# A spectral block with a gated feed-forward layer on one core: filter copies shared out anew, shift columns on ScalarE, special unit and inverse tables moved

## The chip, the core and the metric

One core of a Trainium2 chip. The metric is device time in microseconds (us) of one execution; the median of several runs stands for a kernel. A profile is of one execution, and its span runs from its first to its last instruction. Engines are named as the profile does: PE (TensorE matmul), PEld (its weight loads), DVE (VectorE), ACT (ScalarE), POOL (GpSimd), SP (SyncE, which here only issues DMAs).

## What is computed

With x of 2048 rows and 640 columns, a row c and its modulation vectors sa, ca, ga, sb, cb, gb:

```
sa, ca, ga, sb, cb, gb = split(silu(c) @ w_mod, 6)
h = layernorm(x) * (1 + ca) + sa
x = x + ga * irfft2(rfft2(h) * (w_r + 1j * w_i))
h = layernorm(x) * (1 + cb) + sb
x = x + gb * ((silu(h @ w_gate) * (h @ w_up)) @ w_down)
```

The spectral filter has 2048 x 321 complex values; w_gate and w_up are 640 x 1728, w_down is 1728 x 640. Everything comes and goes as bfloat16.

## The kernel before

The order of the work is written out by hand: each engine runs its instructions in the order in which the Python code issues them, and waits are put in where tiles depend on each other. So moving a line of Python moves an instruction on its own engine's queue.

**Front** (lines 253 to 483). x, the tables and the filters are loaded. The rows are normalized in eight steps t of two tiles (`bn`, `rstd_of`, `normed` on DVE; `normed_pool`, L374, on POOL for the steps and halves that `NP` lists, after `shift` has made a bias). `tok(t)` (L383) transforms along the rows on PE, ACT copies the result out (L386), `ddft(t)` (L324, L327) transforms along the columns, and ACT copies that (L400) into A. One reciprocal square root per step (L359) runs on POOL. `pool_w` issues the eight big filter loads (L276) on POOL's DMA queue: real and imaginary, two column halves, and two directions, `dm` 0 and 1. DMAs of the tables K and the modulation weights are issued by ACT at the end of steps 6 and 7 (L478).

**The filter tile** Wt holds, in each half of 64 partitions (`dm`), 32 partitions that were loaded and 32 partitions that `w_rev` (L319) fills with the same rows, columns reversed. A call takes an engine, `dm` and a range lo to hi of the 82 columns, over all 128 rows k. The calls before: POOL, `dm` 1, 24 to 48; DVE, both, 48 to 64; DVE, both, 64 to 82; DVE, `dm` 0, 0 to 24; ACT, `dm` 0, 24 to 48; DVE, `dm` 1, 0 to 24.

**Groups** (lines 489 to 712). A is turned around in groups of four columns l: groups 0 to 3 are columns 48 to 63, group 4 is column 80 alone (`iE`), then columns 4 to 47 four at a time with the special group 12 (`iS`, "S") among them, group 17 is columns 0 to 3, and groups 18 to 21 are columns 64 to 79; NG is 22. Groups 0 to 4 come through PE transposes (`t2_pe`, copies L530), the others through five DMA transposes on SP (`t2_dma`, L511). `stage_a(g)` makes two matmuls (L542) into one of three pairs of PSUM banks and multiplies both halves by the filter: groups in `MIX` have ACT copy the second half out (L549), DVE multiply the first (L550) and POOL the second (L551); the others are one DVE instruction of twice the size (L553). `stage_c(g)` makes the inverse matmuls (L632, eight for a group of four, in bank g % 2), which ACT copies to E (L633; DVE for groups in `DEV`). The loop at line 688 runs, for round g, `stage_a(g + 2)` and then `stage_c(g - 2)`.

**The special unit** handles row 0 and the Nyquist row. `col0` (L506) has POOL gather one column of each turned group into `Bc`, by the schedule `CZ`; `sa_cols` and `sa_rows` make the shift's own transform; `special_a` (L560, L561) needs all of `Bc`, and the filter's last row k = 127; `special_c` (L570, ACT copy L572) issues four POOL DMAs (L575, L576) into E. `ga_mod` (L638, L643) makes the broadcast ga; `mods` (L580) makes three vectors of modulation columns. After the loop, `s1em` (L653) and `s1er` (L663) transform back along the rows, with the table H, and L1160 and L1163 along the columns with the table RI, which DVE multiplies by ga first (L709, L712). The feed-forward layer follows (lines 715 to 1248).

`idle_pe` (L302) issues matmuls whose result nobody reads.

Of the kernel before, what the change touches and what calls it, by code (L numbers as in the profile page):

```python
# [21 lines left out]
RW = 164  # L22
# [145 lines left out]
def adaln_block_kernel(ctx, tc, A_x, A_w_r, A_w_i, B_x, B_w_gate, B_w_up, B_w_down, c, w_mod, out):  # L168
# [110 lines left out]
    def pool_w(i, n):  # L279
        for ci, mm, dm in wsets[i:i + n]:  # L280
            load_w(nc.gpsimd, ci, mm, dm, *((P - 1, 128, P, -1) if dm else (0, 1, P - 1)))
# [32 lines left out]
                nc.tensor.matmul(ps_ap[:, w * c5:w * c5 + w], lhsT=lhsT, rhs=sc_col[:, k:k + 1].to_broadcast([P, w]),  # L314
                                 start=(k == 0 and c5 == 0), stop=(k == NC5 - 1 and c5 == NC5 - 1))

    def w_rev(eng, dm, lo, hi):
        src = Wt[64 * dm:64 * dm + 32]
        (eng.copy if eng is nc.scalar else eng.tensor_copy)(Wt[64 * dm + 32:64 * dm + 64, :, lo:hi],  # L319
                                                            bass.AP(tensor=src.tensor, offset=src.offset + 160 - lo, ap=[list(src.ap[0]), [RW, P], [-1, hi - lo]]))  # L320

    def dft_d(zps, lhs):
        for h in range(2):
# [6 lines left out]
    if True:  # L330
        CS = (4, 0, 1, 2, 3)
        BA = (1, 3, 5, 7, 11)
        NP = {4: (0,), 5: (0,), 6: (0, 1), 7: (0,)}

        def bn(T, stats=True, aggr=True):
            for k in range(2 * stats):
# [118 lines left out]
        for t in range(2, NS):  # L455
            tok(t)
            if t == 2:
                ddft(0)
            for T in (2 * t + 4, 2 * t + 5):
                if T < NT and T not in BA:  # L460
                    bn(T)
                if T == 2 * t + 4 and t < 7:
                    if t + 1 in NP:
                        shift(t + 1)
                    normed(t + 1, [h for h in range(2) if h not in NP.get(t + 1, ())])
            if t < 7:
                normed_pool(t + 1, NP.get(t + 1, ()))
            if t == 2:
                bn_act(11)
            if t < 5:  # L470
                pool_w(*((4, 2), (6, 1), (7, 1))[t - 2])
            if t < 6:
                rstd_of(t + 2)
            if t == NS - 1:
                idle_pe(3, 4, 3)
            ddft(t - 1)
            for o, i in late.get(t, ()):
                nc.scalar.dma_start(o, i)  # L478
        ddft(7)
        idle_pe(3, 4, 7)  # L480
        w_rev(nc.gpsimd, 1, 24, 48)
        for dm in range(2):
            w_rev(nc.vector, dm, 48, 64)


    Em = rE.cut(0, [64, 128])
# [15 lines left out]
    if True:  # L502
# [11 lines left out]

        for i in range(5):
            t2_dma(i)
        for i in range(1, 4):
            nc.sync.dma_start(wm_r[:, :, i, :], wm_m[:, :, i, :])
        nc.sync.dma_start(Htab[:], H_dram)
        nc.sync.dma_start(RI[:], RI_dram)  # L520
        Wd_sb = rA.cut(0, [NFC, D])

        def t2_pe(slot):
# [68 lines left out]
        def sa_cols(bank):  # L592
            mps = psum[:, bank, 330:330 + NC5]
            mod_cols(mps, wm_sa)
            nc.vector.tensor_copy(sa_col[:], mps)  # L595
            nc.gpsimd.tensor_scalar_mul(sa4[:], mask4[:], sa_col[:, 4:5])
            nc.gpsimd.tensor_copy(_rev(SL, 0, [[257, 4], [132, 2], [16, NS]]),
                                  sa_col[:, 0:4].unsqueeze(2).unsqueeze(3).to_broadcast([P, 4, 2, NS]))
            nc.gpsimd.tensor_copy(_rev(SL, 1024, [[1, 4], [132, 2], [16, NS]]),
                                  sa4[:].unsqueeze(2).unsqueeze(3).to_broadcast([P, 4, 2, NS]))  # L600
# [43 lines left out]


        def s1b(t):
            return 6 if t == 1 else 2 if t == 0 or t % 2 else 4

        def s1em(t, rs=range(4)):
            vps = banks(s1b(t), 2, [8, 128])  # L650
# [13 lines left out]
                                 rhs=Htab[:, t, v, :], start=(v == 0), stop=(v == 1))  # L664
            return vt_copy(t, lo, 5)

        MIX = {g: True for g in range(1, NG - 2) if g % 5 in (1, 2, 4) and g not in (iE, iS)}
        DEV = {NG - 2}
        CZ = {4: (0, 8), 6: (8, 16), 8: (24, 16), 9: (40, 8), 10: (64, 16)}
        PPs = {}  # L670
        t2_pe(0)
        t2_pe(1)
# [1 line left out]
        t2_pe(2)  # L674
        t2_pe(3)
        PPs[1] = stage_a(1)
        w_rev(nc.vector, 0, 64, 82)
        w_rev(nc.vector, 1, 64, 82)
        PPs[2] = stage_a(2)
        sa_cols(0)  # L680
        for s in range(4):
            col0(B2of[groups[s][0]][0], slice(groups[s][0], groups[s][0] + 4)) if s < 3 else None
        B2 = B2of[60][0]
        col0(B2[:, 0:4], slice(60, 64))
        col0(B2[:, 4:5], slice(80, 81))
        w_rev(nc.vector, 0, 0, 24)
        w_rev(nc.scalar, 0, 24, 48)
        for g in range(1, NG + 2):
            if g in CZ:
                l0, n = CZ[g]  # L690
                col0(B2of[l0][0], slice(l0, l0 + n))
            if g + 2 < NG:
                PPs[g + 2] = stage_a(g + 2)
            if g == 1:
                w_rev(nc.vector, 1, 0, 24)
            if g in (3, 4):
                ga_mod(320 * (g - 3), 0)
            if g == 8:
                load_wd()
            if g > 1:  # L700
                stage_c(g - 2)
            if g - 2 == iE:
                sa_rows(iE % 2)
            if g - 2 == iS:
                mods(1, iS % 2)
            if g in (NG - 2, NG - 1):
                mods(g - NG + 4, 2 + 2 * ((g + 2) % 3))
        s1em(0)
        nc.vector.tensor_tensor(RI[:, 1], RI[:, 1], ga_bc[:], ALU.mult)  # L709
        vt_copy(0, 0, 4)  # L710
        s1em(1)
        nc.vector.tensor_tensor(RI[:, 0], RI[:, 0], ga_bc[:], ALU.mult)  # L712
        gdiag = rL.cut(10496, [NC5, 128])

    Wgu = rW.cut(0, [2, NC5, 13 * 128])
# [582 lines left out]
```

## Time and profile before

| | us |
|---|---|
| median of 3 runs | 257.44 (256.94 to 257.88) |
| the profiled execution's own time | 257.12 |
| its span | 255.3 |
| PE busy in the span | 237.0 (93%) |
| DVE busy | 206.8 (81%) |
| ACT busy | 170.2 (67%) |
| POOL busy | 76.0 (30%) |
| mean granted clock of PE | 0.986 |
| front, to the first `t2_pe` matmul (L528) | 0 to 35.73 |
| groups, to the first `s1er` matmul (L663) | 35.73 to 72.11 |
| the rest | 72.11 to 255.3 |

The busy times of engines lie beside each other and do not add up to the span. In the page's second part the span is cut into 40 slices of 6.4 us; a digit is the busy share in tenths, and PEclk is the clock that PE was granted, in tenths. A row of the timeline is start, length, engine, line, operation, output and inputs, how many were merged, and in brackets the time for which the engine stood idle before it and what ended that. A row of stretches gives a window, its length, then busy time and number of instructions of PE, PEld, DVE, ACT and POOL, the granted clock, the DMA engines' busy share and GB/s.

### The profile page before, as it was taken

The page shows a single profiled execution, that of the slowest core. Times are in us where ns is not written, and L with a number is a line of the kernel's source. Part 1 is how long each engine was busy: PE and PEld are TensorE (multiplying, and loading weights), DVE is VectorE, ACT ScalarE, POOL GpSimd, SP SyncE. Part 2 cuts the span into 40 slices and gives each one's busy share as a digit, 9 for nine tenths or more (in the row PEclk, how much of TensorE's full clock was granted, in tenths as well). Part 3 has the DMA queues.
Part 4 walks back from the last instruction along what each step waited for, and adds up shares of the span by engine and source line. Part 5 has one row for each costly group of instructions (what it writes and reads, how often), then busy time and mean ns, then how long its engine had stood idle before and what let it go on. Part 6 is the DMA issues. An engine that isn't in the chain of part 4 may idle for free.

```text
span 255.3 us, 5627 instructions
## 1 busy us (share of the span) xinstructions
PE 237.0 (93%) x2100; PEld 179.4 (70%) x2100; DVE 206.8 (81%) x469; ACT 170.2 (67%) x329; POOL 76.0 (30%) x98
## 2 busy tenths in 40 slices
PE   8678784978999999999999999999999999999994
PEld 2467652556899888778888768888775665656773
DVE  3997379866768999698998996778998788879874
ACT  5988756365789879939876287876336777775220
POOL 4598544464633533200200440000442000003410
PEclk9999999599999999999999999999999999999999
DMA  6999969999998999920000511310511000000111
GB/s 186 347 302 168 161 206 281 168 377 383 209 303 158 282 272 284 181 67 3 0 4 0 103 54 53 25 30 0 105 53 51 3 0 0 4 0 0 55 51 51
DMA packets 40445, 31.78 MB, mean 124 GB/s; under 512 B 22401, under 2 KB 37218, under 8 KB 40290
## 3 DMA queue, kind: packets, MB, share of 16 engines
q1 hardware_dynamic: 35760, 22.35, 32.4%
q0 software_dynamic: 2912, 6.94, 13.3%
q10 hardware_dynamic: 1746, 2.14, 2.8%
q8 instruction: 16, 0.26, 0.4%
q14 instruction: 11, 0.09, 0.1%
HBM read 24.03 MB, written 2.62 MB: 104 GB/s over the span
## 4 chain that ended last, share of the span: by engine, by line
PE 81%; DVE 3%; POOL 2%; ACT 2%; issue 2%; DVEq 0%; POOLq 0%; ACTq 0%
PE psum L1019 35%; PE psum L890 18%; PE psum L989 6%; PE psum L632 3%; PE psum L867 3%; PE psum L653 3%; PE psum L542 3%; PE psum L1160 2%; PE psum L1163 2%; PE psum L977 2%; DVE rW L319 1%; PE psum L638 1%; PE psum L383 1%; POOL rE L551 1%; PE psum L580 1%
## 5 line engine op out<-in xcount | busy, mean ns | idle before, releaser
L1019 PEld LDWEIGHTS <-rW 128*128 128x128 bf16 (+1 forms) x429 | 42.0, 98 | 12.6
L1019 PE MATMUL psum<-rW 128*128 128x256 bf16 (+1 forms) x247 | 42.2, 287 | 0.0
L916 POOL TENSOR_TENSOR rM<-rM,rL 128x320 f32<-128x320 f32 x6 | 5.4, 906 | 96.6 <-ACT rL L915 96.6
L890 PEld LDWEIGHTS <-rE 128*128 128x128 f16 (+1 forms) x196 | 19.0, 97 | 7.8
L890 PE MATMUL psum<-rE 128*128 128x320 f16 (+1 forms) x147 | 22.9, 299 | 0.0
L1057 ACT COPY rX<-psum 128x384 f32<-128x384 f32 (+2 forms) x27 | 14.0, 519 | 7.5 <-PE psum L1019 7.4
L1050 ACT COPY rH<-psum 128x384 f32<-128x384 f32 (+2 forms) x27 | 13.9, 516 | 7.0 <-PE psum L1019 6.3
L1019 PEld LDWEIGHTS <-rE 128*128 128x128 f16 x156 | 15.2, 98 | 4.7
L1054 DVE TENSOR_TENSOR rH<-psum,rM 128x512 bf16<-128x512 f32 (+1 forms) x24 | 15.0, 624 | 4.1 <-PE psum L1019 2.2
L1073 ACT ACTIVATE rL<-psum 128x384 bf16<-128x384 f32 (+2 forms) x27 | 14.4, 532 | 5.5 <-PE psum L1019 3.4
L1058 DVE TENSOR_TENSOR rX<-psum,rX 128x384 f32<-128x384 f32 (+2 forms) x27 | 16.3, 604 | 1.6 <-ACT rX L1057 1.4
L1044 ACT COPY rM<-psum 128x384 f32<-128x384 f32 (+2 forms) x27 | 13.9, 514 | 4.0 <-PE psum L1019 3.9
L633 ACT CAST rE<-psum 127x512 bf16<-127x512 f32 x19 | 11.1, 591 | 7.2 <-PE psum L632 5.7
L632 PEld LDWEIGHTS <-rE 128*128 128x128 bf16 x160 | 11.5, 116 | 6.2 <-issue 3.2
L551 POOL TENSOR_TENSOR rE<-rY,rW 128x512 bf16<-128x512 bf16 x10 | 12.0, 1203 | 12.6 <-ACT rY L549 9.2
L1019 PE MATMUL psum<-rE,rY 128*128 128x256 f16 (+1 forms) x78 | 15.6, 290 | 0.0
L1019 PE MATMUL psum<-rW,rE 128*128 128x256 bf16 (+1 forms) x78 | 15.6, 290 | 0.0
L632 PE MATMUL psum<-rM,rE 128*128 128x128 bf16 (+1 forms) x160 | 12.8, 228 | 2.9 <-DVE sa_col L595 2.4
L1165 DVE SCALAR_TENSOR_TENSOR rM<-psum,rX 128x640 f32<-128x640 f32 x16 | 13.0, 819 | 2.7 <-PE psum L663 1.4
L1074 ACT ACTIVATE rL<-rX 128x384 bf16<-128x384 f32 (+2 forms) x27 | 15.1, 558 | 0.0
L989 PE MATMUL psum<-rW 128*128 128x256 bf16 x130 | 14.5, 273 | 0.0
L383 PE MATMUL psum<-rE 128*128 128x256 bf16 x80 | 10.4, 273 | 4.3 <-ACT rE L386 1.6
(212 smaller groups left out, 639.0 us busy)
## 6 DMA issues: line engine op xcount, KB each, us to landing
out_dram<-rA SPq DMA_DIRECT2D x31, 80.0 KB, 1.6
rM<-in_w_mod_dram SPq DMA_DIRECT2D x3, 800.0 KB, 7.0
rA<-in_B_w_down_dram SPq DMA_DIRECT2D x2, 960.0 KB
rY<-in_B_w_gate_dram POOLq DMA_DIRECT2D x2, 832.0 KB, 7.5
rM<-in_w_mod_dram ACTq DMA_DIRECT2D x2, 800.0 KB, 5.7
rX<-in_A_x_dram SPq DMA_DIRECT2D x4, 320.0 KB, 4.9
rX<-in_A_x_dram SPq DMA_DIRECT2D x2, 640.0 KB, 8.4
rW<-in_B_w_gate_dram SPq DMA_DIRECT2D x2, 640.0 KB
```

Of the source, the lines that this page charges most:

```text
L551: (nc.gpsimd if MIX[g] else nc.vector).tensor_tensor(PP[:, 1], Xs[:], wv[:, 1], ALU.mult)
L632: nc.tensor.matmul(o, lhsT=_rev(pp, P * n * v + j, [[n, P]]), rhs=k(v), start=(v == 0), stop=(v == 1))
L890: nc.tensor.matmul(o, lhsT=lhs[rows(k), k], rhs=rhs[rows(k), k], start=start and k == ks[0], stop=stop and k == ks[-1], skip_group_check=True)
L989: nc.tensor.matmul(gu[u], lhsT=Wgu[:, u, c5, ff * 128:(ff + 1) * 128], rhs=h2T[:, :, c5, :], start=(c5 == 0), stop=(c5 == NC5 - 1))
L1019: nc.tensor.matmul(o[:, f], lhsT=w, rhs=b, start=(start and f == 0 and i == 0), stop=(stop and f == len(groups[g]) - 1 and i == len(ops) - ...
L1044: nc.scalar.copy(c0, X)
L1050: nc.scalar.copy(c2, X)
L1054: nc.vector.tensor_tensor(c11, Z, c0, ALU.add)
L1057: nc.scalar.copy(c3, X)
L1058: nc.vector.tensor_tensor(c22, Y, c3, ALU.add)
L1073: nc.scalar.activation(g21, X, ACT.Silu, scale=-1.0)
L1074: nc.scalar.activation(g22, c22, ACT.Silu, scale=-1.0)
```

## The change

`w_rev` can take a part of the rows (k0 to k1). The calls become: POOL, `dm` 1, 48 to 64 and then 0 to 24; DVE, `dm` 0, 48 to 64; after `stage_a(1)`, DVE, both, columns 80 and 81 of all rows and columns 64 to 79 of the last row alone; after `sa_cols`, DVE, `dm` 0, 0 to 24; and, in the loop by the table `REV`, DVE 24 to 48 of `dm` 0 and 1 (rounds 3 and 4), POOL 64 to 72 and 72 to 80 of both over 127 rows (rounds 6, 8, 11, 14). ACT makes no filter copy any more.

`NP[6]` loses a half: DVE normalizes it in POOL's place. The filter loads 6 and 7 are issued after the step's `rstd_of`. On SP, the tables H and RI are loaded before the last two of three modulation loads. `sa_cols` ends with an ACT copy; what followed it becomes `sa_spread`, one product on DVE and two copies on POOL, in round 1. Two filler matmuls follow `sa_cols`. Group 3 joins `MIX`. `CZ` is a round sooner for four of five blocks. `ga_mod` uses bank 0 and then 1. `special_c` comes in round 13 (14 before) after that round's `stage_c`, the three `mods` come in rounds 19 to 21 after `stage_c` (14, 20 and 21 before), `s1em(0)` and `s1em(1)` come into rounds 22 and 23, `s1em(1)` ahead of the last `stage_c`, and the products of RI into rounds 20 and 21; `s1b` deals the banks of `s1em` out anew.

```diff
-    def w_rev(eng, dm, lo, hi):
+    def w_rev(eng, dm, lo, hi, k0=0, k1=P):
         src = Wt[64 * dm:64 * dm + 32]
...
-        NP = {4: (0,), 5: (0,), 6: (0, 1), 7: (0,)}
+        NP = {4: (0,), 5: (0,), 6: (0,), 7: (0,)}
...
-            if t < 5:
-                pool_w(*((4, 2), (6, 1), (7, 1))[t - 2])
+            if t == 2:
+                pool_w(4, 2)
             if t < 6:
                 rstd_of(t + 2)
+            if 2 < t < 5:
+                pool_w(t + 3, 1)
...
-        w_rev(nc.gpsimd, 1, 24, 48)
-        for dm in range(2):
-            w_rev(nc.vector, dm, 48, 64)
+        w_rev(nc.gpsimd, 1, 48, 64)
+        w_rev(nc.gpsimd, 1, 0, 24)
+        w_rev(nc.vector, 0, 48, 64)
...
-        for i in range(1, 4):
-            nc.sync.dma_start(wm_r[:, :, i, :], wm_m[:, :, i, :])
+        nc.sync.dma_start(wm_r[:, :, 1, :], wm_m[:, :, 1, :])
         nc.sync.dma_start(Htab[:], H_dram)
         nc.sync.dma_start(RI[:], RI_dram)
+        for i in range(2, 4):
+            nc.sync.dma_start(wm_r[:, :, i, :], wm_m[:, :, i, :])
...
-            nc.vector.tensor_copy(sa_col[:], mps)
-            nc.gpsimd.tensor_scalar_mul(sa4[:], mask4[:], sa_col[:, 4:5])
+            nc.scalar.copy(sa_col[:], mps)
+
+        def sa_spread():
+            nc.vector.tensor_scalar_mul(sa4[:], mask4[:], sa_col[:, 4:5])
...
-            return 6 if t == 1 else 2 if t == 0 or t % 2 else 4
+            return 6 if t == 1 else 4 if t == 0 or t % 2 else 2
...
-        MIX = {g: True for g in range(1, NG - 2) if g % 5 in (1, 2, 4) and g not in (iE, iS)}
+        MIX = {g: True for g in range(1, NG - 2) if (g % 5 in (1, 2, 4) or g == 3) and g not in (iE, iS)}
         DEV = {NG - 2}
-        CZ = {4: (0, 8), 6: (8, 16), 8: (24, 16), 9: (40, 8), 10: (64, 16)}
+        CZ = {4: (0, 8), 5: (8, 16), 7: (24, 16), 8: (40, 8), 9: (64, 16)}
+        REV = {3: ((nc.vector, 0, 24, 48),), 4: ((nc.vector, 1, 24, 48),), 6: ((nc.gpsimd, 0, 64, 72),), 8: ((nc.gpsimd, 1, 64, 72),),
+               11: ((nc.gpsimd, 0, 72, 80),), 14: ((nc.gpsimd, 1, 72, 80),)}
...
-        w_rev(nc.vector, 0, 64, 82)
-        w_rev(nc.vector, 1, 64, 82)
+        for dm in range(2):
+            w_rev(nc.vector, dm, 80, 82)
+            w_rev(nc.vector, dm, 64, 80, LP, P)
         PPs[2] = stage_a(2)
         sa_cols(0)
-        for s in range(4):
-            col0(B2of[groups[s][0]][0], slice(groups[s][0], groups[s][0] + 4)) if s < 3 else None
+        idle_pe(2, 4, 1)
+        w_rev(nc.vector, 0, 0, 24)
+        for s in range(3):
+            col0(B2of[groups[s][0]][0], slice(groups[s][0], groups[s][0] + 4))
...
-        w_rev(nc.vector, 0, 0, 24)
-        w_rev(nc.scalar, 0, 24, 48)
         for g in range(1, NG + 2):
...
+            for w in REV.get(g, ()):
+                w_rev(*w, *((0, LP) if w[2] > 63 else ()))
             if g == 1:
-                w_rev(nc.vector, 1, 0, 24)
+                sa_spread()
             if g in (3, 4):
-                ga_mod(320 * (g - 3), 0)
-            if g == 8:
+                ga_mod(320 * (g - 3), (g - 1) % 2)
+            if g == 9:
                 load_wd()
-            if g > 1:
+            if g in (NG - 2, NG - 1):
+                nc.vector.tensor_tensor(RI[:, NG - 1 - g], RI[:, NG - 1 - g], ga_bc[:], ALU.mult)
+            if g == NG + 1:
+                s1em(1)
+            if g > 1 and g - 2 != iS:
                 stage_c(g - 2)
+            if g == NG:
+                s1em(0)
+                vt_copy(0, 0, 4)
+            if g - 1 == iS:
+                stage_c(iS)
             if g - 2 == iE:
                 sa_rows(iE % 2)
-            if g - 2 == iS:
-                mods(1, iS % 2)
-            if g in (NG - 2, NG - 1):
-                mods(g - NG + 4, 2 + 2 * ((g + 2) % 3))
-        s1em(0)
-        nc.vector.tensor_tensor(RI[:, 1], RI[:, 1], ga_bc[:], ALU.mult)
-        vt_copy(0, 0, 4)
-        s1em(1)
-        nc.vector.tensor_tensor(RI[:, 0], RI[:, 0], ga_bc[:], ALU.mult)
+            if NG - 3 <= g < NG:
+                mods(g - NG + 4, 7 if g == NG - 2 else 5)
```

## The prediction, made before the changed kernel was run

> **What bounds the kernel now.** I read the page's slices first, then busy time by stretch, the chain that ended last, and the timeline of VectorE (DVE) and GpSimd (POOL) between 26 and 73 us. The page's second part shows where TensorE is not full and where its clock falls:
>
> ```profile
> PE   8678784978999999999999999999999999999994
> ...
> PEclk9999999599999999999999999999999999999999
> ```
>
> From 72.5 us on TensorE is full (the stretch 90 to 255 us has PE busy 161.92 of 165), so what the middle saves before the first `L663` matmul at 72.11 us is saved at the end. By stretch:
>
> ```profile
> 37.00:40.00 3.00, 1.69 (x14) 0.93 (x13) 2.91 (x5) 1.10 (x2) 0.00 (x0) 1.00 1.05 367
> 42.00:45.00 3.00, 0.60 (x7) 0.49 (x6) 2.92 (x5) 2.32 (x1) 1.42 (x2) 0.76 1.29 245
> 45.00:48.00 3.00, 3.00 (x16) 1.70 (x15) 2.91 (x4) 0.62 (x2) 1.92 (x9) 0.50 0.75 144
> ```
>
> The busy columns are PE, PEld, DVE, ACT, POOL, then the clock. DVE is full (2.9 of 3) while PE is not; after the hole PE is full only because its clock is halved. The chain, between 37 and 45 us, names DVE's filter copies (L319):
>
> ```profile
> 37.61 0.74 DVE rW L319
> ...
> 41.09 0.98 DVE rW L319
> 42.08 1.70 DVE rW L319
> 43.85 0.57 issue
> 44.42 0.17 DVE sa_col L595
> 44.63 1.01 PE psum L632 x8
> ```
>
> The timeline says why those copies are long and where PE waits later:
>
> ```profile
> 34.17 2.77 POOL L319 COPY rW<-rW 32x3072 bf16<-32x3072 bf16 x1 [4.07 <-DMA rW<-in_A_w_i_dram]
> 35.41 2.94 DVE L319 COPY rW<-rW 32x2048 bf16<-32x2048 bf16 x2
> 41.09 2.69 DVE L319 COPY rW<-rW 32x2304 bf16<-32x2304 bf16 x2
> 41.59 1.51 POOL L551 TENSOR_TENSOR rE<-rY,rW 128x512 bf16<-128x512 bf16 x1 [0.20 <-ACT rY L549]
> 57.61 0.20 POOL L506 COPY rY<-rW 128x16 bf16<-128x16 bf16 x1
> 57.87 0.20 PE L560 MATMUL psum<-rY,rM 128*128 128x81 bf16 x1 [1.68 <-POOL rY L506]
> 65.82 2.31 POOL L551 TENSOR_TENSOR rE<-rY,rW 128x512 bf16<-128x512 bf16 x2
> ```
>
> Three things. POOL cannot begin on the filters before their DMA lands, about 34.1 us. DVE's filter copies and POOL's instructions take turns: the first DVE copy of 2048 elements takes 2.15 us and ends 0.62 us after POOL's ends at 36.94, the second, alone, 0.76; the pair at 41.09 has one behind a product that ends at 41.39 and one behind the product that ends at 43.10, each done 0.68 later. And PE waits 1.68 us at 57.87 for the special unit's last column copy on POOL.
>
> **Front, 26 to 34 us.** POOL's second normalization (L374, two in 1.74 us) goes to DVE at 0.44; DVE has room (1.86 busy of 26 to 30). The statistics' power (L359, 0.70) no longer stands behind a DMA issue (1.12). PE's transform at 28.21 waited for that pair; it could start near 26.7, when ScalarE's copy frees the banks. ScalarE's two copies per step (1.23 each) then set the pace, and I get the last transform 1.4 us sooner (29.3 for 30.74). The two DMA issues moved behind the power start 0.8 and 0.4 us later; issue to landing is a median of 11.5 us for this tensor, so they stand in a backlog and I cost this at nothing (if the last one lands 0.4 later, POOL's list below is 0.4 later). Because the landing does not move, the 1.4 us helps PE and DVE, not POOL.
>
> **POOL's list, 34 to 54 us.** ScalarE loses a copy of 2.79, DVE the two of 2304 and one of 2048 (2.69 with waits, and 0.76), and gains four tiny ones and one of 3072 (1.02 alone). POOL gets 2048 and 3072 elements at once, and four pieces of 127 x 8 later. By elements, 2.77/3072 = 0.90 ns: 1.85, 2.77 and 0.92 each. A piece is not in the trace: if nothing but rows counted it would be 127/128 of 2.77 = 2.75; from below, the column copy of 128x16 takes 0.20. I take 0.92, because the nearest row with short rows (L551, four elements a row) takes 1.15 for 512 elements of two inputs, which leaves no room for a price per row.
>
> Now POOL in the new order, with the DVE copies that take turns with it: DVE 2048 0.62; POOL 1.85 + 2.77; two products 2.30; four tiny DVE copies 0.6 (estimate: 0.15 each as for the 128x5 copy; 0 if they don't contend, 1.7 at the 0.42 of DVE's 512-element copy L530); five column copies 0.68; DVE 3072 0.89; product 1.15; the two shift spreads 0.45 + 0.55; column 0.19; product 1.15; DVE 3072 0.89; column 0.21; product 1.15; DVE 3072 0.89; piece 0.92; column 0.21; product 1.15; column 0.17; piece 0.92; column 0.20. Sum 19.9, from 34.17 to 54.1. Nothing in it waits for PE, if the clock holds. PE's special products, 57.87 before, start at 54.1: **3.8 us sooner**. On the way PE still waits: its fifth stage-A pair needs the bank that DVE's product of group 2 frees, near 43 us, since the tiny copies stand between two POOL products; and stage A of group 10 needs DVE's product of group 7, near 51.1. These are new waits in the place of the 2.40, 0.98 and 0.85 us of before, and they end no later than POOL's list.
>
> The rest of this stretch lies beside it: the shift columns on ScalarE (0.15 on DVE before) and the mask product on DVE (POOL's 1.12 was spent behind a DVE copy) take both off POOL's path; the ga products' other bank removes a wait of 0.51; two filler matmuls (0.27 each, three in 0.81) fall in PE's idle time, and cost 0.5 if that is gone.
>
> **After 54.1.** PE: special products 0.31, stage C 0.45, three rounds of A and C at 0.88, special stage C 0.30: 57.8. ScalarE's copy 0.24 with its wait, then POOL: four DMA issues 2.28, product 1.15, piece 0.92, product 1.15 = 5.5, to 63.8. That is when stage C of group 17 may start (67.1 before; PE alone would be ready near 61.9, so this is a new wait of some 2 us). Moving the special stage C one round forward put its DMA issues ahead of two more products; before, POOL did these at 65.82 and PE hardly waited. Then PE: 0.55, three vectors of modulation columns at 0.60, stage C 4 x 0.45, first inverse transforms 16 matmuls 0.90 = 5.05, and ScalarE's copy of the last group 0.73 with its wait, now exposed: 5.8, to 69.6. Before, the same stretch took 72.11 - 67.11 = 5.0, as one modulation vector lay earlier (62.55) and the inverse transforms hid the copy. **Sum: 67.1 - 63.8 = 3.3, less 0.8: 2.5 us faster.** The table of the inverse transform moved ahead of two modulation loads on SP costs nothing: loads of 7.0 us median, with the last needed after 65 us. The multiplications of RI (0.48 each) stay beside PE.
>
> Against the profiled execution, 257.12: 254.6. The median of the runs shown is 257.44, 0.32 above it; the same step from there is 254.9, my figure.
>
> **The clock.** It fell to 0.50 between 43 and 44 us, 1 to 2 us into an idle time of 2.40, after a stretch in which PE was busy little and with one-column matmuls; matmul groups then took 0.85 for 0.43. In the new order PE has holes of about 1.7 (37 to 38.7) and 1.4 us (41.7 to 43), so by this row it may fall again, sooner. Then groups up to 47 us take double; the product of group 6 comes 1.5 us later on POOL, of which some 0.8 is taken up by a DVE copy that goes in the gap: 0.7 us lost of the 2.5.
>
> [...]
>
> **Rivals.** (1) The clock falls, and POOL is later by this and by a filter landing 0.4 later: gain 2.5 - 0.7 - 0.4 = 1.4, 256.0. For it: the holes; against: fillers, and the front's gain. (2) POOL is shorter than I sum: the tiny copies don't contend (0.6 to 0), and PE's wait behind the four DMA issues is filled, since the products before them start sooner: up to 2 more, 252.9. For it: idle POOL time of nearly 1 us at 56 to 57 in my order; against: POOL's products and copies alone are 26 us of the 31 from 34 to 65. (3) **Slower**: the pieces cost by the row. At 2.75 for 0.92 the four, all ahead of the product of group 17, add 7.3, less 1 us of POOL's idle time: 257.44 - 2.5 + 6.3 = 261.2. It decides from a piece of about 0.92 + (2.5 + 1)/4 = 1.8 us on. Against it: L551's row. (4) The change's parts cancel: POOL's list takes the place of DVE's, with both the clock and an estimate of 1 us missed: within 0.8 us of before.
>
> **Chances.** Forecast (gain 1.9 to 3.2) 0.36; rival 1 (0.8 to 1.9) 0.19; rival 2 (over 3.2) 0.17; rival 4 (no change) 0.12; rival 3 0.16. A measurement tells 0.3% (0.8 us) from no change: faster 0.72, same 0.12, slower 0.16. The range leaves out the far part of rival 2 (0.04) and rival 3 (0.16): 252.6 to 257.9.
>
> **What would show it.** POOL busy from 34.2 to 54 with hardly a gap; pieces near 0.92; special products near 54; PE idle some 2 us before stage C of group 17, put down to POOL; first `s1er` matmuls near 69.6; no idle on ScalarE's filter copy any more. I am wrong if PE waits for DVE instead at 57 to 64, if the pieces take over 1.8, or if anything after 72 us stretches, where I assume that all loads (the gate and up weights above all) keep pace.

## The result and the profile after

The changed kernel takes **258.44 us** (median of 12 runs, 257.02 to 261.41); the kernel before, on the same chip, 256.9 us. The ratio is 1.0068, with a 95% interval of 1.0039 to 1.0097: slower by 0.7%, where 254.9 us was forecast. (Here and in the table below, a run over 1.5% above the fastest of its kernel is left out of the ratio, one each of kernels 2 and 15 and four of kernel 10, while medians and ranges count every run.) The profiled execution took 257.83 us (span 256.0, mean granted clock 0.987), 0.7 us more than the profiled execution of before.

The slices of the changed kernel (PE, POOL, granted clock):

```profile
PE   8578976787999999999999999999999999999994
...
POOL 4599479889224543200200440000442000003410
PEclk9999999999679999999999999999999999999999
```

POOL works longer (84.6 us for 76.0; between 32 and 60 us 23.6 for 12.9), as forecast. But the place where the clock falls has moved: from slice 8 (43.5 us) to slices 11 and 12 (66 to 73 us). The timeline has the marks of the forecast:

```profile
33.68 5.17 POOL L319 COPY rW<-rW 32x2048 bf16<-32x2048 bf16 x2 [4.54 <-DMA rW<-in_A_w_i_dram]
...
38.82 2.77 DVE L319 COPY rW<-rW 32x256 bf16<-32x256 bf16 x4
...
38.94 2.39 POOL L555 TENSOR_TENSOR rE<-rY,rW 128x512 bf16<-128x512 bf16 x2
...
49.49 1.73 POOL L319 COPY rW<-rW 32x1016 bf16<-32x1016 bf16 x1
52.82 1.05 POOL L319 COPY rW<-rW 32x1016 bf16<-32x1016 bf16 x1
54.19 0.20 PE L564 MATMUL psum<-rY,rM 128*128 128x81 bf16 x1 [0.33 <-POOL rY L509]
64.47 0.25 PE L638 MATMUL psum<-rM,rE 128*128 128x64 bf16 x1 [1.03 <-POOL rE L555]
72.53 0.40 PE L669 MATMUL psum<-rH,rE 128*128 128x128 bf16 x2 [0.25 <-ACT rE L639]
```

The special products start at 54.19 (57.87 before; 54.1 forecast) and the second half of stage C of group 17 at 64.47 (63.8 forecast). Then the forecast breaks: the first `s1er` matmul (L669, L663 before) comes 8.06 us later, not 5.8, at 72.53. The same row of the kernel before:

```profile
71.95 0.28 PE L663 MATMUL psum<-rH,rE 128*128 128x128 bf16 x2
```

(The 72.11 given ahead of the result is from the chain, which counts the matmul from the end of the one before it; all times here are from timelines.) So the 3.7 us won at the special products are gone 18 us later, and 0.6 us more. After the first `s1er` matmul the spans differ by 0.1 us (183.4 before, 183.5 after).

The two longest waits of PE between 30 and 74 us (total, times, longest):

```profile
PE psum L546 <- DVE rE L554: 4.1, 4, 1.5
PE psum L638 <- POOL rE L555: 1.7, 2, 1.0
```

Stage A waits for a bank that DVE's product frees, and stage C of group 17 for POOL's product. Cut into stretches of 3.41 us that begin where the clock falls (here with PE's busy time alone, then clock, DMA share and GB/s), first of the kernel before, then of the changed one:

```profile
40.12:43.53 3.41, 1.71 (x30) 1.00 1.29 240
43.53:46.95 3.42, 2.32 (x13) 0.50 0.99 210
46.95:50.36 3.41, 3.41 (x18) 0.50 1.07 175
```

```profile
62.86:66.27 3.41, 2.29 (x53) 1.00 1.11 282
66.27:69.69 3.42, 3.42 (x71) 0.50 1.25 225
69.69:73.10 3.41, 3.16 (x31) 0.50 1.09 348
```

Both have 6.83 us at half clock, each after a stretch in which PE did little. In the changed kernel that stretch holds the longer of the two waits for POOL (1.03 us) and the first vectors of modulation columns, 25 matmuls of one column each: 0.77 us of the timeline for 25 columns, where the matmuls of 512 columns start 0.21 us apart at full clock. The row counts both as busy.

### The profile page after: what moved, and what is told of

Same layout as the page of the kernel before. It is cut to its first block, busy times and chain, and to the rows that moved or that the text cites. A ratio compares the mean times of both kernels' runs of the same rounds, so it can differ in the third digit from the quotient of the medians.

```text
span 256.0 us, 5640 instructions
## 1 busy us (share of the span) xinstructions
PE 237.3 (93%) x2102; PEld 180.8 (71%) x2102; DVE 208.6 (81%) x472; ACT 168.5 (66%) x330; POOL 84.6 (33%) x102
## 4 chain that ended last, share of the span: by engine, by line
PE 77%; POOL 6%; DVE 5%; ACT 2%; issue 1%; DVEq 0%; POOLq 0%; ACTq 0%
PE psum L1032 35%; PE psum L903 18%; PE psum L1002 5%; PE psum L659 3%; PE psum L880 3%; PE psum L638 2%; POOL rE L555 2%; PE psum L1173 2%; PE psum L1176 2%; POOL rW L319 2%; PE psum L990 1%; PE psum L546 1%; DVE rW L319 1%; PE psum L384 1%; DVE bn6a L338 1%
## 5 line engine op out<-in xcount | busy, mean ns | idle before, releaser
L638 PE MATMUL psum<-rM,rE 128*128 128x128 bf16 (+1 forms) x160 | 14.0, 233 | 2.5 <-POOL rE L555 1.7
L872 DVE TENSOR_TENSOR rA<-psum,rM 128x320 bf16<-128x320 f32 (+1 forms) x27 | 12.1, 471 | 2.4 <-PE psum L880 2.3
L1002 PEld LDWEIGHTS <-rW 128*128 128x128 bf16 x130 | 12.7, 98 | 1.7 <-issue 0.2
```

The lines of the kernel that those rows point to most:

```text
L638: nc.tensor.matmul(o, lhsT=_rev(pp, P * n * v + j, [[n, P]]), rhs=k(v), start=(v == 0), stop=(v == 1))
L1002: nc.tensor.matmul(gu[u], lhsT=Wgu[:, u, c5, ff * 128:(ff + 1) * 128], rhs=h2T[:, :, c5, :], start=(c5 == 0), stop=(c5 == NC5 - 1))
```

## The experiments

The theory at first was that this half clock at the end of the groups is the loss; the rivals, that the pieces on POOL, DVE's copies, or the end's new order cost time themselves. "Filler" means calls of `idle_pe`.

| kernel | median us (range) | ratio to before (95%) |
|---|---|---|
| the changed kernel | 258.44 (257.02 to 261.41) | 1.0068 (1.0039 to 1.0097) |
| 1 changed, filler at the end | 256.51 (255.67 to 258.32) | 0.9999 (0.9969 to 1.0028) |
| 2 changed, last piece on ACT | 256.43 (255.09 to 262.17) | 0.9987 (0.9954 to 1.0019) |
| 3 before, filler in the hole | 254.96 (254.27 to 256.08) | 0.9924 (0.9896 to 0.9952) |
| 4 changed, one `mods` early | 256.78 (254.87 to 257.97) | 0.9976 (0.9946 to 1.0005) |
| 5 as 3, and the change's front | 255.0 (254.63 to 257.07) | 0.9950 (0.9928 to 0.9971) |
| 6 before, the change's end | 258.26 (256.82 to 259.6) | 1.0065 (1.0038 to 1.0092) |
| 7 as 1, all pieces on ACT | 256.76 (256.14 to 258.32) | 1.0014 (0.9991 to 1.0038) |
| 8 changed, copies as before | 253.8 (253.72 to 254.88) | 0.9908 (0.9884 to 0.9933) |
| 9 before, the change's copies | 259.61 (258.18 to 260.52) | 1.0101 (1.0055 to 1.0147) |
| 10 changed, no pieces | 256.78 (253.72 to 258.07) | 0.9935 (0.9895 to 0.9975) |
| 11 as 8, with the pieces | 256.97 (256.7 to 259.38) | 1.0031 (1.0 to 1.0061) |
| 12 as 8, fillers at 37 to 40 us | 256.5 (254.69 to 257.3) | 0.9970 (0.9940 to 1.0001) |
| 13 as 10, half of w_down later | 254.49 (253.36 to 256.9) | 0.9935 (0.9901 to 0.9968) |
| 14 as 8, one `mods` early | 253.71 (252.93 to 254.23) | 0.9876 (0.9841 to 0.9911) |
| 15 as 8, half of w_down later | 254.66 (253.41 to 257.65) | 0.9917 (0.9894 to 0.9940) |
| 16 as 8, and the end as before | **253.28** (252.71 to 255.0) | 0.9879 (0.9841 to 0.9917) |
| 17 as 10, once more | 257.73 (one run) | |
| 18 as 10, one `mods` early | 255.84 (252.94 to 256.28) | 0.9929 (0.9896 to 0.9962) |

Every run also has a mean granted clock. One stretch of 3.41 us at half clock makes it about 0.993, two make it about 0.987 (by half of 3.41 and of 6.83 us in a span of 255). The kernel before, over all its runs beside these experiments, has a median of 255.9 us at 0.993 (38 runs) and of 257.1 at 0.985 to 0.987 (68 runs), so in it a stretch costs some 1.1 us. The mean tells how long the clock was half, not where. Seven runs of the changed kernel lie at 0.985 to 0.987, with a median of 257.9: at the same mean clock it is 0.9 us slower than before. Four more of its twelve runs lie at 0.980 or below, which is rare in the kernel before (nine of 129).

### The clock: 1, 2, 3, 4

Kernel 1 puts five matmuls of 512 columns into PE's wait ahead of stage C of group 17:

```diff
+            if g == NG - 3:
+                idle_pe(5, 4, 4)
```

> The changed kernel with five more filler matmuls on PE ahead of stage C of group 17, where PE waits 1.0 us for POOL's product. Theory (the clock): the change loses because PE's clock halves from 66.3 to 73.1 us after a stretch of little matmul work; then the fillers hold the clock at 1.00, the first s1er matmuls come near 70.3 instead of 72.5, and the median falls by about 2.2 us, to some 256.2. Rival (the queue alone): POOL's product of group 17 and the longer order behind it set the end whatever the clock; then nothing moves (258.4), or the fillers cost up to 0.2.

256.51 us, 1.9 less than the changed kernel. In its profile the same stretch, and the mark after it:

```profile
62.86:66.27 3.41, 3.20 (x57) 1.00 1.10 290
```

```profile
70.44 0.28 PE L669 MATMUL psum<-rH,rE 128*128 128x128 bf16 x2 [0.45 <-ACT rE L639]
```

The clock stays at 1.00, stage C of group 17 starts at 64.48, 0.01 from the changed kernel, and the first `s1er` matmul follows 5.96 us later (5.8 forecast). So 2.1 us of the time from stage C of group 17 to the first `s1er` matmul is the clock. The other runs agree: seven of twelve have a mean clock of 0.997 or more, where the changed kernel has none above 0.992. But 256.51 is only level with the kernel before: something else is lost.

Kernel 2 moves the piece ahead of group 17's product to ACT: `14: ((nc.scalar, 1, 72, 80),)`.

> The changed kernel with the filter piece of round 14 (columns 72 to 80, dm 1) made by ACT in POOL's place. Rival (the queue alone): the product of group 17 comes 1.05 us sooner, near 63.4, and the median falls by just that, to about 257.4. Theory (the clock): the wait ahead of stage C of group 17 nearly goes, so the clock may hold as well; then the fall is 1.05 + 2.2, to about 255.2. If the clock falls all the same, both say 257.4.

256.43 us, between the rival's 257.4 and the theory's 255.2: the wait for POOL ahead of group 17 is gone, and the profiled execution has a full clock at the end, but half clock at 11.36 and 42.08 us instead. Kernel 3 is the kernel before with eight fillers in its own hole:

```diff
+            if g == 2:
+                idle_pe(8, 4, 1)
```

> The kernel before with eight filler matmuls on PE ahead of stage C of group 0, in the wait of 2.40 us at 42.2. Theory (the clock): the half clock from 43.5 to 50.4 goes, and with it up to 2.9 us of matmul time; DVE's and POOL's queues take part of that, so the median falls by 1 to 2.5 us, to 254.5 to 256. Rival (the queue alone): DVE's and POOL's queues set this stretch and the clock adds nothing: 256.9.

254.96 us, 2.0 less than before. So the half clock at 43.53 had cost the kernel before as much as the one at 66.27 costs the changed one. With both holes filled, the changed order is 1.5 us slower than the old one (256.51 against 254.96). Kernel 4 returns the first `mods` to round 13, so that it is not in the low stretch:

```diff
-            if NG - 3 <= g < NG:
+            if g - 1 == iS:
+                mods(1, iS % 2)
+            if NG - 2 <= g < NG:
```

> The changed kernel with the first of the three modulation vectors made in round 13, behind the special stage C, instead of round 19. Rival (the queue and the order alone): 0.6 us of matmuls leave the tail and lie in the later wait for POOL, so the median falls by 0.6, to 257.8. Theory (the clock): as the clock falls after this wait, the vector's 0.8 us at half clock goes from the tail, and the fall is 0.8 with the clock still halved; if the shorter run of one-column matmuls lets the clock hold, 0.6 + 2.2 (255.6).

256.78 us, again between the two; in the profile the end is at full clock and half clock stands at 10.74 and 41.46. Taking the cause away at one place does not keep the clock full at the others.

### Which part of the change costs: 5, 6, 7, 8

Kernel 5 is kernel 3 with the change's `NP` and order of `pool_w`.

> The kernel before with the eight fillers of the run before it (e3, 254.96) and the change's front: one normalization from POOL to DVE and two filter loads issued behind the power. Theory (POOL waits for the filters): transforms end 1.0 us sooner, but POOL's first filter copy waits for its DMA at about 34 us all the same, so the median gains 0 to 0.5: 254.5 to 255.0. Rival (the front counts in full): 1.0 less, 254.0.

255.0 for 254.96: by the medians nothing. The two profiled executions, both with half clock from 10.5 or 10.9 us on, do differ, by 1.1 us at the first `s1er` matmul. The mean clocks tell why the medians don't: ten of kernel 5's twelve runs lie at 0.993 or below, three of kernel 3's eleven. At 0.991 to 0.993 the medians are 255.0 (eight runs) and 255.8 (three), so at the same clock the front gains some 0.8 us. Why kernel 5's clock fell more often is not shown. Kernel 6 is the kernel before with the change's end: special stage C in round 13, `mods` in 19 to 21, `s1em` and RI in the loop.

> The kernel before with the change's end of the groups alone: special stage C in round 13, modulation vectors in rounds 19 to 21, inverse transforms and the products of RI inside the loop, banks dealt anew. Theory (POOL's longer list makes PE wait, and the wait halves the clock): without the filter pieces POOL is not late for group 17, the clock holds after 60 us, and the order alone costs the 0.6 us of a vector moved into the tail: 257.0 to 257.6, with the clock still halved at 43.5. Rival (the order of the end is to blame): PE's clock falls in the tail here too, near 66 us, and the median is 2 us up, some 259.

258.26, 1.4 us more than before. Six runs lie where the theory had them or just below (256.8 to 257.6 us, clock 0.987 to 0.993), six near the rival's 259 (258.9 to 259.6, clock 0.978 to 0.986); the three at 0.993 have a median of 256.9, 1.0 more than before at that clock. The first `s1er` matmul of the profiled execution (256.86 us), 6.5 us after group 17's stage C (4.8 before) at full clock, and the copy that its row names:

```profile
70.49 0.58 ACT L633 CAST rE<-psum 127x512 bf16<-127x512 f32 x1 [0.31 <-PE psum L632]
...
71.67 0.27 PE L663 MATMUL psum<-rH,rE 128*128 128x128 bf16 x2 [0.99 <-ACT rE L633]
```

One more `mods` lies here (0.6 us), and the inverse transforms no longer cover ACT's copy. But the copy ended at 71.07, and PE went on at 71.67: the last 0.6 us are no wait for ACT. They fit the stop that kernels 8 and 12 show (below; 0.59 and 1.20 us), at the same place of PE's stream. Kernel 7 is kernel 1 with `nc.scalar` for `nc.gpsimd` in all four pieces.

> The changed kernel with the five fillers ahead of stage C of group 17, and all four eight-column pieces made by ACT in POOL's place. Theory (POOL's list is the bound from 34 to 64 us): 3.9 us of pieces go from the list, the special unit comes near 52.5 and stage C of group 17 near 61.5, and the median falls by 1.5 to 2.5 from e1's 256.5, to 254 to 255. Rival (DVE's queue or ACT's bounds it as much): under 0.7 less than e1, 255.8 to 256.5.

256.76, above what either gave: no gain over kernel 1. PE still waits 4.1 us in four waits for DVE's L554. POOL's list alone is not what holds the middle. Kernel 8 undoes the new sharing of the copies and leaves the rest of the change:

```diff
-        w_rev(nc.gpsimd, 1, 48, 64)
-        w_rev(nc.gpsimd, 1, 0, 24)
-        w_rev(nc.vector, 0, 48, 64)
+        w_rev(nc.gpsimd, 1, 24, 48)
+        for dm in range(2):
+            w_rev(nc.vector, dm, 48, 64)
...
-            w_rev(nc.vector, dm, 80, 82)
-            w_rev(nc.vector, dm, 64, 80, LP, P)
+            w_rev(nc.vector, dm, 64, 82)
...
+        w_rev(nc.scalar, 0, 24, 48)
...
+            if g == 1:
+                w_rev(nc.vector, 1, 0, 24)
```

> The changed kernel with the filter copies shared out as in the kernel before, and all else as changed. Theory (POOL's list): POOL's copies of 2.77 + 1.85 + 4 x 1.05 shrink to 2.77, group 17's product is not late and the clock holds after 60 us; but DVE's long copies stand at 41 us again, so PE's hole there and its half clock return: about 257. Rival (the end's order): the copies do not matter to the loss, and it stays at 258.4.

**253.8 us**, below both kernels and outside what either theory gave. Its waits and marks:

```profile
PE psum L546 <- DVE rM L534: 2.3, 2, 1.5
```

```profile
53.15 0.20 PE L564 MATMUL psum<-rY,rM 128*128 128x81 bf16 x1
...
68.20 0.28 PE L659 MATMUL psum<-rH,rE 128*128 128x128 bf16 x2 [0.59 <-issue]
68.44 0.27 PE L669 MATMUL psum<-rH,rE 128*128 128x128 bf16 x2
```

The waits for DVE's L554 are gone, and the special products come even 1.0 us sooner than with the copies that were to speed them up. By the medians the new sharing costs 4.6 us, and the rest of the change is a gain of 3.1; by the ratios it is 4.1 and 2.4. At a mean clock of 0.993 four of its runs took 253.7 to 253.9, 2.1 less than before, so part of the 3.1 is that the clock fell less.

### Which copies: 9, 10, 11

Kernel 9 is the kernel before with the new sharing alone.

> The kernel before with the new sharing of the filter copies and nothing else of the change. Theory: the sharing is itself the loss, since DVE and POOL take turns in 38 to 52 us whatever stands at the end of the groups: it costs here what its undoing gave in the changed kernel (258.4 to 253.8 us), so 259 to 261 us, with a new PE wait on DVE's product of the first halves of several us. Rival: the sharing costs only together with the later order of the end, because only there PE waits for the product of group 17: here 256 to 257.5 us, and the special products some 2 us sooner than 57.87 without any gain at the first s1er matmul.

259.61, 2.7 us more than before: the time of the theory, but not its wait, as PE does not wait for DVE's product of the first halves. Its special products wait longer for POOL than in any other kernel:

```profile
57.02 0.20 PE L561 MATMUL psum<-rY,rM 128*128 128x81 bf16 x1 [3.23 <-POOL rY L507]
```

Kernel 10 gives columns 64 to 81 back to DVE (`w_rev(nc.vector, dm, 64, 82)`, and `REV` only with rounds 3 and 4); kernel 11 is its counterpart, kernel 8 with the tiny copies and pieces.

> The changed kernel with columns 64 to 81 filled by DVE in two copies of 2304 elements after stage_a(1), as before; no tiny copies on DVE, no pieces on POOL; the rest of the new sharing (POOL's two copies first, DVE's 24 to 48 in rounds 3 and 4) stays. Theory A: the tiny copies (2.77 us for four, by turns with POOL) and the pieces (four at 1.05 us ahead of the product of group 17) are the loss: 254 to 255.5 us, PE hardly waiting ahead of stage C of group 17. Theory B: DVE's two copies in rounds 3 and 4, which stand ahead of the products that PE waits for (4.1 us in four waits), are the loss: 257.5 to 259 us, with those waits still there.

> The changed kernel with all copies as before (253.8 us) but for columns 64 to 81, which are filled by the tiny copies on DVE and the pieces on POOL as the change does. The counterpart of the run without pieces. Theory A (tiny copies and pieces are the loss): 256 to 258.5 us. Theory B (the copies in rounds 3 and 4 are the loss): 253.5 to 254.8 us, as the tiny copies give back DVE's 2.69 us.

Kernel 11: 256.97, 3.2 us more than kernel 8: theory A. Its waits:

```profile
PE psum L564 <- POOL rY L509: 2.2, 1, 2.2
PE psum L638 <- POOL rE L555: 1.7, 2, 1.0
```

The pieces (1.05 us each) and tiny copies put the special products 2.0 us later (55.14), and with the waits ahead of group 17 the first `s1er` matmul 3.0 us later (71.39). Kernel 10's runs lie in two groups, 253.7 to 254.6 and 256.6 to 258.1, so its median of 256.78 says little, and its ratio leaves out four runs of the upper group; its lower group lies where kernel 8's runs lie, although PE still waits 3.3 us for L554. So most of the loss is the pieces and tiny copies; DVE's two copies in rounds 3 and 4 leave waits that a run may or may not pay for.

### The best kernel, and what spreads the runs: 12 to 18

Kernel 12 fills kernel 8's holes at 37 and 39 us: `idle_pe(4, 4, 1)` ahead of `stage_a(1)` and `idle_pe(2, 4, 1)` after it.

> The changed kernel with the copies as before (253.8 us), and with four filler matmuls of 512 columns in PE's idle time of 1.48 us at 37 us (ahead of stage A of group 1) and two in that of 0.85 us after it. Theory: the half clock of 3.41 us at 41.0 us, which stood in all of that kernel's runs, comes of these holes; filled, it goes, and PE gains 0.4 to 1.2 us: 252.6 to 253.4 us, clock 1.00 from 34 to 72 us. Rival: the clock falls anyway or later, or PE's own work there waits for DVE all the same: 253.6 to 254.5 us.

The profiled execution has the clock of 1.00 that the theory wanted, and took 254.81 us; ten of the twelve runs have a mean clock of 0.993 or less, and the median is 256.5. So the fillers did not keep the clock full, and even at full clock there was no gain. The profile shows something else, a stop in the middle of eight matmuls of one line, with nothing waited for:

```profile
66.70 0.39 PE L638 MATMUL psum<-rM,rE 128*128 128x128 bf16 x4
68.28 0.41 PE L638 MATMUL psum<-rM,rE 128*128 128x128 bf16 x4 [1.20 <-issue]
```

Kernel 8 has such a stop at 68.20 (above), between two L659 matmuls: twelve instructions further in the program, and kernel 12 has exactly twelve more ahead of it (six fillers and their weight loads). In both it stands after PE's 1212th record (matmuls, loads and the sequencer's own), and it ends 1.5 us after the end of a packet of the instruction queue (65.6 to 66.6 and 65.7 to 66.8 us), sent while the DMA engines were full (share over 1.0). So I took it that PE waited for a block of its own instructions that landed late. That is a guess from these times: whose instructions a packet holds, and what sends it, no view shows. Kernels 13 and 15 load the second half of w_down (960 KB) after the first gate and up loads instead of ahead of them; kernel 14 makes kernel 4's edit on kernel 8, which spreads PE's instructions.

> The kernel without pieces, with the second half of the down weights (960 KB) loaded after the first gate and up loads in place of before them. Theory: the runs of that kernel near 257.5 us, against those near 253.9, come of an instruction block of PE that lands late: in the profiles of three kernels PE stops for 0.6 to 1.2 us near 67 to 68 us at the same place of its instruction stream (the 1212th record of matmuls and weight loads), with nothing that it waits for, and the instruction queue's only packet in that stretch runs at 65.7 us, while the DMA engines are full. With 960 KB less ahead of it, the packet runs before 64.5 us, the stop goes, and the times draw together at 253 to 254 us. Rival: the queue in which the block stands is filled anyway by the other loads, or the cause is the clock: two clusters as before, median 255.5 to 257 us, packet at 65 us or later.

> The changed kernel with the copies as before (253.8 us), with the first of the three vectors of modulation columns back in round 13. Theory of the instruction block: 50 of PE's instructions come 6 us sooner, so the block's request comes about 1 to 2 us sooner while PE reaches its first instruction at about the same time: the stop of 0.6 us at 67.6 us goes, 253.0 to 253.6 us. Rival: it is no block of instructions but the inverse matmul's own operand: the stop stays at the first s1em matmuls of the second step, 253.7 to 254.3 us.

> The changed kernel with the copies as before (253.8 us), with the second half of the down weights loaded after the first gate and up loads. Theory: as in the kernel without pieces, the block lands sooner and the stop of 0.6 us goes: 253.0 to 253.6 us. Rival: no difference, or a loss, because the row transposes that follow on SP's queue start later than 76.8 us or DVE's folding of gb into the down weights waits for the late half: 253.8 to 256 us, with an idle time on those rows.

Kernels 13 and 15: the rival. Their packets run at 65.9 and 66.2 us and PE stops for 1.4 and 1.3 us (the median of kernel 13, 254.49, lies in neither's range). Kernel 14: no stop, as the theory had it. Its median of 253.71 is kernel 8's within the noise, and in the rival's range; but at a mean clock of 0.993 its two runs took 252.9 and 253.0, kernel 8's four 253.7 to 253.9, about the 0.6 us of the stop less. The instruction queue's packet falls into the stretch 65 to 66 us in kernel 8 and 64 to 65 in kernel 14 (count, MB, share), which reaches the place later, too:

```profile
q8 instruction: 1, 0.02, 6.7%
```

```profile
q8 instruction: 1, 0.02, 7.2%
```

> The changed kernel with the copies as before (253.8 us), and with the end of the groups in the order of before as well (special stage C in round 14, modulation columns in rounds 14, 20 and 21, inverse transforms and products of RI after the loop): of the change only the front, the special unit's sooner columns, the shift columns on ScalarE, the other bank and the fillers are left. Theory: those are what gains, and the end's new order is a loss of its own, as on the kernel before (258.3 for 256.9): 252.5 to 253.5 us. Rival: the end's new order is what gains once the copies don't stand in its way: 254.5 to 256 us.

Kernel 16, **253.28 us**, lies in the theory's range. It is the change without its copies and without its end. Against kernels 8 and 14 (0.9908, 0.9876; 0.9879 here) the intervals overlap: the end's order neither loses nor gains there beyond what can be told, so that the theory's second half, a loss by the end's order, is not shown. (At 0.993 its two runs took 252.7 and 253.0, as kernel 14's.) What is left of the change gains 1.2% on before (3.1 us by the ratio, and as much at that clock): the front, the special unit's sooner columns, the shift columns on ACT, the banks, group 3 in `MIX`, the two fillers and the order of the loads on SP. Only the front was run by itself (kernel 5).

Kernels 17 and 18 ask what spreads kernel 10's runs: the same kernel with another profile, and with one `mods` early.

> The kernel without pieces once more, for the profile of one execution that may be of the kind near 257.5 us (the profiled one before took 253.9). Theory: with the clock held through 37 to 48 us, a window of half clock falls near the end of the groups, 60 to 72 us, where all of it is paid for, with the late instruction block on top: first s1er matmul 2 to 3.5 us later than 68.70. Rival: the clock is full there, and the instruction block alone lands later: a stop of over 2 us at the 1212th record. If the execution is of the kind near 253.9 us, neither is told apart.

> The kernel without pieces, with the first of the three vectors of modulation columns back in round 13, which removed the stop at the 1212th record in the kernel with the copies as before. Theory of the instruction block: no run near 257.5 us any more, all within 253 to 254.5 us. Rival (the clock's window at the end of the groups): runs of 256.5 to 258 us stay, about as many as before (half).

The new profile is of 257.73 us, against 253.91 of the first. Neither theory holds: the stop is 0.8 us and the clock full from 60 us on; it fell at 11.12 and 41.84 us. The stretches of this execution, and of the first at nearly the same places:

```profile
7.71:11.12 3.41, 1.49 (x13) 1.00 1.06 381
11.12:14.53 3.41, 3.41 (x38) 0.50 1.05 392
38.43:41.84 3.41, 1.32 (x13) 1.00 1.13 320
41.84:45.25 3.41, 3.41 (x37) 0.50 1.30 242
```

```profile
8.31:11.72 3.41, 1.99 (x17) 1.00 1.07 383
11.72:15.13 3.41, 3.41 (x47) 1.00 1.04 393
```

The same instructions, cut 0.6 us apart, and once the clock falls and once not. The first `t2_pe` matmul is 1.65 us later (36.36 for 34.71) and the special products 3.6 (56.99 for 53.41). Kernel 18 keeps half of its runs at 256.1 to 256.3 us though its profile has no stop: the stop does not make those runs. Its profile, of 256.18 us, has half clock at 11.00 and 41.72 too. The length of the half clock does not by itself tell kernel 10's groups apart: one run of the lower group has a mean clock of 0.991, and three of the upper have 0.993. Where it falls may decide; that is not shown.

## Why the prediction was wrong

- **Front**: right in kind. The last transform came at 29.71 (forecast 29.3), and POOL's start was fixed by the filter's landing (4.54 us of idle time), which itself came 0.5 sooner.
- **POOL's list, 34 to 54 us**: right in sum (54.19 for 54.1), partly by luck: it began 0.5 sooner and took 20.5 us, not 19.9. A piece took 1.05 (0.92 taken; the one of 1.73 holds a turn of DVE's copy, which the sum had apart, at 0.89). POOL also stood idle for 0.61 us until DVE's mask product and for 0.74 until ACT's copy, where the sum had no wait. The term of the tiny copies lay on the wrong engine: the four took 2.77 us of DVE's time (bound 1.7), while POOL's two products beside them took 2.39 for the 2.30 of the sum, so POOL lost next to none of the 0.6. The rival of pieces by the row (2.75 each) did not come.
- **"They end no later than POOL's list"**, said of the new PE waits for DVE: they did not delay the special products. But kernels 8 and 11 show that the list itself was the wrong thing to lengthen: with the copies as before the products start at 53.15, and POOL's product of group 17 is not late either (of the two waits for POOL only the earlier one, 0.65 us, is left). I compared the new list with the old one, 57.87, and never with the same change without the new copies.
- **After 54.1**: stage C of group 17 at 64.47 for 63.8, and a wait ahead of it put down to POOL, as said (1.68 us in two parts).
- **The step that failed: "then PE ... 5.8, to 69.6".** It is 5.96 at full clock (kernel 1) and was 8.06, since the clock was half from 66.27 to 73.10. The difference to the forecast of 69.6 is 2.93 us: 0.67 from POOL, 0.16 in this stretch, 2.10 from the clock. "The clock" was weighed for 37 to 47 us only, although the forecast itself put a new wait of 2 us and three vectors of one-column matmuls at this place. None of the four rivals had this: rival 1 had the clock fall, but earlier and for 0.7 us, and rival 3 was slower by the price of the pieces. At full clock the sum held better: kernel 1's profiled execution took 255.67, 1.1 more than the forecast's 254.6 for it. But the median of kernel 1's seven runs at 0.997 or more is 256.3, 1.4 above 254.9, and 0.6 of that no row accounts for.
- **A sum against a base that held the same cost**: the 72.11 us of before (71.95 by the timeline, which makes the gain to 69.6 2.35 and the same stretch of before 4.8) contain 6.83 us of half clock, worth 2.0 us (kernel 3). The slower half-clock matmuls at 45 to 48 us were shown and not priced. By this count a forecast of 2.5 us was mostly the clock's recovery, which the new order spent again elsewhere. With both holes filled the new order is 1.5 us slower, and kernels 8, 9 and 11 put that on the new copies.
- **The rest of the kernel** kept pace, as assumed (0.1 us).

Open: where in the program the half clock lies in the runs without a profile, and so how much of the changed kernel's spread (257 to 261 us, by the mean clocks 4.1 to 17.1 us of half clock) each place makes; what parts kernel 10's runs; why kernel 12's clock fell in most runs in spite of its fillers; and the price of the end's order apart from clock and stop.

## What to carry to other kernels

Price the half clock that stands in the time before, and look in the new order for every stretch of some 3.4 us in which PE streams few columns, one-column matmuls counted as nothing (0.22 and 0.25 of the stretch at full clock, in the kernel before and the changed one); closing one such hole and opening another won nothing here. Compare a new sharing of copies with the rest of the change made without it: here one part gave some 3 us and another took more than 4, and the first sum hid both. Two runs of the same kernel 3.8 us apart (253.91 and 257.73) are worth a second profile before the difference is called noise.

## What the runs showed of the hardware

- **Half clock began on a grid of 3.41 us.** In the kernel before the clock was half from 43.53 to 50.36 us (6.83, twice 3.413), then full for 204.80 us (60 times), until 255.16; in the changed kernel half from 66.27 to 73.10 (6.83). In every profile here with more than one half-clock stretch, the stretches begin whole multiples of 3.413 us apart (in kernel 17 11.12 and 41.84: 9.00; in kernel 9 43.73 and 57.39: 4.00), and where this grid lies against the program differs between executions (kernels 2, 4, 17 and 18 have half clock from 11.36, 10.74, 11.12 and 11.00 us on).
- **Ahead of a half-clock stretch PE had streamed few columns.** Cut the profiles by this grid, and take the columns that the matmuls of a window would stream at full clock (a 512-column matmul as 0.21 us, as the trace has them start 0.215 us apart, a one-column one as nothing, each in the window in which it starts) as a share of the window. Over all windows of the 20 profiles that end between 8 and 240 us: after a full-clock window filled by less than 0.30, the next was at half clock in 8 of 8 cases; from 0.30 to 0.36 in 7 of 13; to 0.41 in 5 of 24; above that in none of 1,289. (The profiles of before and after alone: 2 of 2, 0 of 1, 0 of 1, 0 of 128.) Ahead of 66.27 us in the changed kernel it was 0.25, though PE counts as busy for 0.67 of it and the longest wait there was 1.03 us; ahead of 43.53 in the kernel before 0.22.
- **PE stopped at one place of its stream, with no wait that the profile shows.** With the groups' end packed, it stopped for 0.5 to 1.4 us at its 1212th to 1217th record (as some are missing) in kernels 2, 6, 7, 8, 10, 12, 13, 15 and 17, until 1.3 to 1.7 us after the end of an instruction packet of 16 KB sent while the DMA engines were full (share 1.02 to 1.27). In the other eleven profiles PE came to that place 1.5 us or more after the packet's end, and did not stop. That PE lacked instructions there is my reading of these times; whose instructions a packet holds is not in the profile.
- Even the smallest DVE copies between filter partitions were longer beside POOL's products: in the changed kernel two of 32x256 and two of 32x16, beside two POOL products, took 2.77 us for the four, and 1.94 in kernel 11. One copy of 32x16 took 1.14 us and ended 0.03 after the first product (40.19), where the other took 0.16.
